# A kernel's index stores: which VectorE operation each waits for, and how far apart they are planned

## The chip, the core and the metric

The kernel runs on one core of one Trainium2 chip. The metric is the device time of one execution in microseconds; the number that stands for a kernel is the median of several executions.

## What is computed

The kernel does two things in a row: a DeltaNet attention block, and a router with two of eight experts for every token.

```python
# attention: B, H, S, D = 4, 8, 768, 48
k_n = k / (norm(k) + 1e-06)
for t in range(S):
    y[:, :, t] = einsum('bhd,bhde->bhe', q[:, :, t], state)
    v_old = einsum('bhde,bhd->bhe', state, kt)
    state = state + bt * einsum('bhd,bhe->bhde', kt, vt - v_old)
# router and experts: x is y as 3072 tokens x 384; E = 8 experts, F = 1024
noisy_logits = x @ w_gate + log1p(exp(x @ w_noise)) * noise
top2 = argpartition(-noisy_logits, 2, axis=1)[:, :2]
top2_w = softmax over the two
for e in range(E):
    out[mask_e] += top2_w[mask_e] * (maximum(x[mask_e] @ w1[e], 0) @ w2[e])
```

The recurrence over tokens is done in chunks of 64 tokens, so that it becomes small matmuls and the inversion of small triangular matrices. Which tokens an expert gets depends on the data, so the tokens' rows are sorted by expert in DRAM: a list `tokens_x` says, for every place of every expert, the token's number, its weight and where its row of `x` lies.

## The kernel before

**Attention.** There are 24 units: 6 steps of 4 units, a unit being one chunk of 64 tokens of two batch entries with all 8 heads. For a unit, TensorE turns k and q (L614), multiplies k by k, q by k and the state by k (`by_token`, L630), reads the state with q (L903), solves for the new values (L948), adds up the state (L970), finishes the answer (L1007), turns it (L1017) and multiplies it by the router's weights (L1022). GpSimd scales v by the norms of k (L912). VectorE masks the product of q and k (`within`, L882), subtracts what the state already gives from v (`recur`, L932), adds the new state (`add_state`, L982), and inverts the triangular matrices of a step: a column at a time, a product (L761) and an addition (L765). ScalarE copies most results out of PSUM. The rows of the answer are stored to `rows_y` by SP (`store`, L399).

**Routing.** When all steps of a group are through (3, 2 and 1 steps: `ROUTES`), `route` works out for its tokens both experts, both weights and both places in `tokens_x` (the last of it is the cast to integers at L1153). Then the lists are stored: for each unit and each of the two experts one indirect DMA by GpSimd writes 128 entries of 12 bytes to their places in `tokens_x` (`spread`, L441). These are the *index stores*: 24 for the first group, 16 for the second, 8 for the last, 48 in all.

**Early experts.** Expert 0's weights fit beside the attention. After steps 2 and 4, SP loads the first entries of expert 0's list (`early_rows`, `early_meta`, L1278), which waits for the stores of these steps; GpSimd gathers those tokens' rows (`take_rows`, L405); and TensorE computes expert 0 for them (`early`, L1322, L1343, L1367), two tiles of 128 tokens as batch 1, then three as batch 2.

**Experts.** After the attention, `rest` does what is left of expert 0 (L1731 to L1757), and experts 1 to 7 follow (L1591 and L1702). For each, GpSimd gathers rows, adds up weights (L1557) and adds the results to the output in DRAM (L460).

**What sets the order.** The attention, the routing and the early experts aren't emitted in the order of the code. Every operation is a job with an engine, an estimated cost, the things it reads and writes, and perhaps a due time. `Jobs.order` plans all of them on a model of the five engines and returns them by planned start; then they are emitted in this order, and each engine's queue runs them in it, GpSimd's and SP's too. Before the plan, due times are handed back from a job to what it needs. Jobs with `apart` may not be planned to start closer together than that: `spaced` holds the earliest start of the next such job. Index stores of the first two groups have `apart=jobs.APART` (L1231), the last group's have none (`paced` is false for the last step).

**What a store waits for.** `spread` gets a list `behind` and makes the store wait for each instruction in it ("not all of them at once", L452). The list is `columns`, which `column` (L765) replaces with the addition of the inversion's column that was emitted last. So a store waits until VectorE has done the last column operation planned ahead of it. Once the last inversion has been emitted, the list no longer changes.

Of the kernel before, what the change touches and what calls it, by code (L numbers as in the profile page):

```python
# [100 lines left out]
class Jobs:  # L101
# [122 lines left out]
        return sorted(done, key=lambda job: job.start)  # L224

    AFTER = -20
    APART = 1.6
    PATIENCE = 0.112
    SOON = 44.8

# [7 lines left out]
def kernel(  # L238
# [39 lines left out]
    nc = tc.nc  # L278
# [191 lines left out]
    def deltanet(ictx):  # L470
# [6 lines left out]
            [psum.tile([128, 2, 512], FP32, name=f"pair{i}") for i in range(3)],  # L477
        )
        PE, ACT, DVE, POOL, SP = Jobs.ENGINES

        def bank(size, ahead=False):

            if size == 2:
                return Bank(2, (0, 1) if ahead else (0, 1, 2))
            return Bank(1, (0,) if ahead else (0, 1))
# [55 lines left out]
        def t_invs(g):  # L541
            return t_two[g % 2]
# [82 lines left out]
        def by_token(out, to, kT, rhs):  # L625

            for j in range(NP):
                for b in range(2):
                    for z in range(2):
                        nc.tensor.matmul(  # L630
                            out[to(z, b), z, j], kT[rows_of[z], j, crossed(z, b)],
                            rhs(z, j, b), start=(j == 0), stop=(j == NP - 1),
                            skip_group_check=True,
                        )
# [52 lines left out]
        def invert(g):  # L687

            first_s, steps = INVERSIONS[g]
            t, v_ = t_invs(g)[:, 0:steps], nc.vector  # L690
            t_key, d_key, n_key, ss_key, root_key = (
                (x, g % 2) for x in ("t", "d", "norm", "ss", "root")
            )
            diagonal = t.rearrange("p s i j -> p s (i j)")[:, :, 0 : Q * Q : Q + 1]
            ss, root, norm, d, minus_d = (x(g)[:, 0:steps] for x in small.values())
            shape = [128, steps, Q, Q]
            soon = FIRST + first_s * PACE + 2 * steps + 1.0
            per = 1.06 * steps

            def squares():  # L700
                v_.tensor_copy(ss, diagonal)
                v_.tensor_scalar_max(root, ss, 1e-30)

            def by_log():
                nc.scalar.activation(root, root, ACTF.Ln)
                nc.scalar.activation(root, root, ACTF.Exp, scale=0.5)

            def lengths():


                v_.reciprocal(norm, root)
                v_.tensor_tensor(out=norm, in0=norm, in1=ss, op=ALU.mult)
                v_.tensor_tensor(out=norm, in0=norm, in1=root, op=ALU.add)
                v_.tensor_scalar(
                    out=norm, in0=norm, scalar1=0.5, scalar2=1e-6, op0=ALU.mult, op1=ALU.add
                )
                v_.tensor_tensor(out=d, in0=norm, in1=norm, op=ALU.mult)
                v_.reciprocal(d, d)
                v_.tensor_tensor(
                    out=d, in0=d, in1=beta_b[:, first_s : first_s + steps], op=ALU.mult  # L720
                )
                v_.tensor_scalar_mul(minus_d, d, -1.0)

            jobs.add(DVE, 0.4, squares, reads=[t_key], writes=[ss_key, root_key], due=soon)
            jobs.add(ACT, 0.5, by_log, writes=[root_key], due=soon + 1)

            for x in range(steps):
                jobs.add(
                    POOL, 1.5,
                    lambda x=x: [nc.gpsimd.affine_select(  # L730
                        out=t[:, x], in_=t[:, x], pattern=[[1, Q], [-1, Q]], base=0,
                        channel_multiplier=0, compare_op=ALU.is_gt, fill=0.0,
                    )],
                    reads=[ss_key], writes=[t_key], due=soon + 3,
                )
            every_beta = [("beta", i) for i in range(128 // H)]
            jobs.add(
                DVE, 2.0, lengths, reads=[root_key, ss_key, *every_beta], writes=[n_key, d_key],
                due=soon + 3,
            )  # L740
            for x in range(steps):
                jobs.add(
                    DVE, 0.2,
                    lambda x=x: v_.transpose(out=norms(first_s + x), in_=norm[:, x]),  # L744
                    reads=[n_key], writes=[("norms", first_s + x)],
                )
            jobs.add(
                DVE, 0.15 + per,
                lambda: v_.tensor_tensor(
                    out=t, in0=t, in1=minus_d[:, :, None, :].to_broadcast(shape), op=ALU.mult  # L750
                ),
                reads=[d_key], writes=[t_key],
            )


            def column(j):
                shape = [128, steps, Q - 1 - j, j]
                part = parts[:, 0 : steps * shape[2] * j].rearrange(
                    "p (s i j) -> p s i j", s=steps, j=j
                )  # L760
                v_.tensor_tensor(  # L761
                    out=part, in0=t[:, :, j + 1 :, j, None].to_broadcast(shape),
                    in1=t[:, :, None, j, 0:j].to_broadcast(shape), op=ALU.mult,
                )
                columns[:] = [v_.tensor_tensor(  # L765
                    out=t[:, :, j + 1 :, 0:j], in0=t[:, :, j + 1 :, 0:j], in1=part, op=ALU.add
                ).ins]

            for j in range(1, Q - 1):
                jobs.add(  # L770
                    DVE, 0.36 + 0.0019 * steps * j * (Q - 1 - j), lambda j=j: column(j),
                    writes=[t_key, *(("column", first_s + x, j) for x in range(steps))],
                )
            jobs.add(DVE, 0.2, lambda: v_.memset(diagonal, 1.0), writes=[t_key])
            jobs.add(
                DVE, 0.15 + per,
                lambda: v_.tensor_tensor(
                    out=t, in0=t, in1=d[:, :, :, None].to_broadcast(shape), op=ALU.mult
                ),
                reads=[d_key], writes=[t_key],  # L780
            )
# [86 lines left out]
        def within(n):  # L868

            turned(n, "q", qps, NQ, qTs, NQ)  # L870
            p = bank(2, True)
            jobs.add(
                PE, 0.6,
                lambda: by_token(
                    two_banks(p, C), crossed, kTs(n),
                    lambda z, j, b: qTs(n)[rows_of[z], j, rows_of[b]],
                ),
                reads=[("kT", n % NT_), ("qT", n % NQ)], opens=p, lands=2.0,
            )
            jobs.add(  # L880
                DVE, 0.7,
                lambda: nc.vector.tensor_tensor(  # L882
                    out=qks(n), in0=two_banks(p, C),
                    in1=mask[:, None, None, :].to_broadcast([128, 2, NP, C]), op=ALU.mult,
                ),
                writes=[("qk", n % NQ)], closes=p,
            )

        def recur(n):
# [29 lines left out]
            if c:  # L919
                p_b = bank(2)  # L920
                jobs.add(
                    PE, 0.5,
                    lambda: by_token(
                        two_banks(p_b, D), straight, kTs(n),
                        lambda z, j, b: old[rows_of[z], b, j],
                    ),
                    reads=[("kT", n % NT_), ("st", z, c % N_ST)], opens=p_b,
                )
                r = by_parity(v_n)
                jobs.add(  # L930
                    DVE, 0.58,
                    lambda: nc.vector.tensor_tensor(  # L932
                        out=r, in0=r, in1=two_banks(p_b, D), op=ALU.subtract
                    ),
                    writes=v_key, closes=p_b,
                )
                jobs.add(
                    PE, 0.55, of_state,
                    reads=[("qT", n % NQ), ("qk", n % NQ), ("st", z, c % N_ST)],
                    writes=[("of_state", z)], opens=p_y,  # L940
                )
# [37 lines left out]

            def add_state():  # L980
                if c:
                    nc.vector.tensor_tensor(  # L982
                        out=new, in0=two_banks(p_s, D), in1=old, op=ALU.add
                    )
                else:
                    nc.vector.tensor_copy(new, two_banks(p_s, D))

# [71 lines left out]
                writes=[("logits", turn_r % 2, at + i)], closes=p_xt,  # L1059
            )  # L1060

        columns = []
        small = {
            x: ring([128, most_steps, Q], x, 2) for x in ("ss", "root", "norm", "d", "minus_d")
        }
# [12 lines left out]
        def route(g):  # L1078
# [141 lines left out]
            for x in range(units):  # L1220
                of, i = first_s + x // US, x % US
                for y, to in enumerate(slot):
# [7 lines left out]
                        due=FIRST + (s + paced) * PACE + BEHIND + jobs.AFTER,  # L1230
                        apart=jobs.APART * paced,  # L1231
                    )
# [693 lines left out]
```

## Time and profile before

| | |
|---|---|
| median of 3 runs | 830.22 us (827.91, 830.22, 830.33) |
| profiled execution: its own time | 829.14 us |
| profiled execution: span from the first to the last instruction | 827.3 us |
| TensorE busy | 732.1 us, 88% of the span |
| VectorE, ScalarE, GpSimd busy | 541.8, 308.6 and 418.5 us |
| mean granted TensorE clock | 0.877 of full |
| index stores (L441): issue time on GpSimd | 48, 48.5 us, 1010 ns each |
| gathers of rows for experts (L405, `xr`) | 49, 55.7 us, 1138 ns each |
| stretch of the first group's stores | 216 to 279 us |
| second and last group's stores | 299 to 320 us, 347 to 357 us |
| batch 1 and batch 2 of the early experts on TensorE | 331 to 353 us, 353 to 386 us |

How to read it: times on a page are microseconds of one profiled execution from the start of its span. An engine's name stands for its queue; "L1591" is the line of the kernel. PE is TensorE, PEld its weight loads, DVE is VectorE, ACT is ScalarE, POOL is GpSimd and SP issues DMAs. In the slices of the span each digit is the busy share of one fortieth, 20.7 us, in tenths, and the row PEclk is the clock that TensorE was granted, in tenths of full speed. In a timeline a row ends with how long the engine was idle before it and what ended that. "issue" means that the engine waited for nothing that the profile shows. "remote" is a semaphore event whose sender the profile doesn't name. One matmul of the program shows as two in the trace.

### The profile page before, as it was taken

Reading aid. Unit: us, or ns where it says so; the run is one execution under the profiler, and the core shown is the slowest. Engines: PE = TensorE matmul, PEld = TensorE weight load, DVE = VectorE, ACT = ScalarE, POOL = GpSimd, SP = SyncE. Lnnn points to the kernel's source line nnn. Section 1 sums busy time; section 2 is a strip of 40 time slices with the busy share of each in tenths; the row PEclk is TensorE's granted clock in tenths of the full one; section 3 lists DMA queues with packets and bytes.
Section 4 is the critical chain, followed back from the end, with each engine's and each line's share of the span. In section 5 each row is a group of like instructions: output and inputs, shape, how many; then the busy total and the mean of one; then the engine's idle time right before and its main releaser. Section 6 shows DMA issues by size and latency. Waiting matters only on the chain.

```text
span 827.3 us, 22382 instructions
## 1 busy us (share of the span) xinstructions
PE 732.1 (88%) x9319; PEld 572.1 (69%) x9319; DVE 541.8 (65%) x1100; ACT 308.6 (37%) x728; POOL 418.5 (51%) x408
## 2 busy tenths in 40 slices
PE   5656879898887875999999999999999999999993
PEld 3445768687776765777659668678588587596593
DVE  7999968998762240302588488487586686785831
ACT  3758485856442621222250250430520521501500
POOL 5030031021245343359678777786886886787032
PEclk8556886987575775999999999999999999999997
DMA  4456544322433100525834545444544446333031
GB/s 70 89 99 179 137 130 97 85 61 61 128 70 89 51 23 12 191 60 90 199 103 118 119 113 122 127 111 100 148 148 75 120 139 128 88 61 42 2 39 24
DMA packets 142719, 79.60 MB, mean 96 GB/s; under 512 B 118352, under 2 KB 139024, under 8 KB 141584
## 3 DMA queue, kind: packets, MB, share of 16 engines
q1 hardware_dynamic: 125840, 57.25, 26.6%
q0 software_dynamic: 12800, 19.80, 13.4%
q8 instruction: 75, 1.23, 0.6%
q10 hardware_dynamic: 3968, 1.03, 0.6%
q14 instruction: 36, 0.29, 0.1%
HBM read 49.85 MB, written 20.03 MB: 84 GB/s over the span
## 4 chain that ended last, share of the span: by engine, by line
PE 65%; DVE 15%; issue 11%; POOL 3%; ACT 2%; SPq 2%; DMA 1%; another core or an unknown queue 0%; POOLq 0%; DVEq 0%; ACTq 0%
PE inner L1591 25%; PE outer L1591 14%; DVE w2e L761 5%; PE pair L1343 3%; PE pair L1367 3%; PE pair L630 3%; DVE w1e L765 3%; POOL out_dram L460 2%; DVE w2e L765 2%; PE pair L903 2%; PE inner L1702 2%; PE single L1022 2%; PE pair L948 2%; PE pair L1007 2%; PE pair L970 1%
## 5 line engine op out<-in xcount | busy, mean ns | idle before, releaser
L1658 ACT ACTIVATE hT<-inner 128x416 f32<-128x416 f32 x112 | 57.8, 517 | 260.9 <-PE inner L1591 258.1
L1652 DVE TENSOR_TENSOR hT<-hT,inner 128x416 f32<-128x416 f32 x182 | 105.5, 586 | 63.5 <-PE inner L1591 55.4
L460 POOL DMA_INDIRECT out_dram<-sums,metas_x x51 | 83.4, 1635 | 93.0 <-DVE sums L1491 67.3
L441 POOL DMA_INDIRECT tokens_x<-meta,slot x48 | 48.5, 1010 | 63.4 <-DVE w2e L765 25.9
L1591 PE MATMUL inner<-s_x,w1e 128*128 128x416 f32 x196 | 78.7, 512 | 0.0
L912 POOL TENSOR_TENSOR v<-v,norms 128x384 f32<-128x384 f32 x24 | 23.4, 988 | 104.8 <-DVE norms L744 49.9
L405 POOL DMA_INDIRECT xr<-rows_y,metas_x x49 | 55.7, 1138 | 19.1 <-issue 12.8
L1647 ACT ACTIVATE hT<-hT 128x416 f32<-128x416 f32 x112 | 59.9, 547 | 12.1 <-DVE hT L1652 7.0
L1591 PEld LDWEIGHTS inner<-s_x,w1e 128*128 128x128 f32 x196 | 37.2, 190 | 31.2 <-issue 28.8
L1591 PE MATMUL inner<-xe,w1e 128*128 128x416 f32 x140 | 58.1, 513 | 0.0
L1591 PE MATMUL outer<-t_w,hT 128*128 128x192 f32 x336 | 58.0, 326 | 0.0
L1591 PE MATMUL inner<-s_x,s_w 128*128 128x416 f32 x140 | 56.9, 512 | 0.0
L1591 PEld LDWEIGHTS outer<-t_w,hT 128*128 128x128 f32 x336 | 55.2, 190 | 0.0
L1557 POOL TENSOR_TENSOR w1e<-w1e 128x256 f32<-128x256 f32 x63 | 52.7, 846 | 2.4
L1591 PE MATMUL outer<-w2e,hT 128*128 128x192 f32 x280 | 50.7, 328 | 0.3
L1591 PEld LDWEIGHTS outer<-w2e,hT 128*128 128x128 f32 x280 | 46.1, 190 | 4.3 <-issue 2.1
L1591 PEld LDWEIGHTS inner<-s_x,s_w 128*128 128x128 f32 x140 | 26.6, 190 | 22.3 <-issue 22.3
L819 ACT COPY w<-tt_tb 32x256 f32<-32x256 f32 x96 | 38.6, 402 | 7.1 <-DVE tt_tb L796 3.9
L1591 PEld LDWEIGHTS inner<-xe,w1e 128*128 128x128 f32 x140 | 26.4, 190 | 20.7 <-issue 17.0
L1591 PE MATMUL outer<-t_w,s_h 128*128 128x192 f32 x224 | 40.6, 329 | 0.0
L1487 DVE TENSOR_SCALAR sums<-outer,metas_x 128x192 f32<-128x192 f32 x70 | 27.8, 410 | 18.4 <-PE outer L1591 17.8
L1591 PEld LDWEIGHTS outer<-t_w,s_h 128*128 128x128 f32 x224 | 36.6, 190 | 4.2 <-issue 4.2
(202 smaller groups left out, 1611.3 us busy)
## 6 DMA issues: line engine op xcount, KB each, us to landing
w1e<-in_moe_w_dram SPq DMA_DIRECT2D x8, 1536.0 KB
w2e<-in_moe_w_dram SPq DMA_DIRECT2D x8, 1536.0 KB
v<-in_v_dram SPq DMA_DIRECT2D x48, 96.0 KB
qp<-in_q_dram SPq DMA_DIRECT2D x48, 96.0 KB
out_dram<-empty SPq DMA_DIRECT2D x4, 1152.0 KB
rows_y<-y SPq DMA_DIRECT2D x24, 192.0 KB
xq<-xr SPq DMA_DIRECT2D x52, 84.0 KB
kp<-in_k_dram SPq DMA_DIRECT2D x88, 48.0 KB
```

The source lines that it names most:

```text
L405: d = nc.gpsimd.indirect_dma_start(out=got, out_offset=None, in_=rows_y[0 : units * 128], in_offset=bass.IndirectOffsetOnAxis(ap=index, ax ...
L441: d = nc.gpsimd.indirect_dma_start(out=tokens_x, out_offset=bass.IndirectOffsetOnAxis(ap=slot, axis=0), in_=meta, in_offset=None, bounds_c ...
L460: d = nc.gpsimd.indirect_dma_start(out=out, out_offset=bass.IndirectOffsetOnAxis(ap=index, axis=0), in_=got, in_offset=None, bounds_check= ...
L761: v_.tensor_tensor(out=part, in0=t[:, :, j + 1 :, j, None].to_broadcast(shape), in1=t[:, :, None, j, 0:j].to_broadcast(shape), op=ALU.mult,)
L765: columns[:] = [v_.tensor_tensor(out=t[:, :, j + 1 :, 0:j], in0=t[:, :, j + 1 :, 0:j], in1=part, op=ALU.add).ins]
L819: lambda rows=rows, cols=cols, w64=w64, tt=tt: nc.scalar.copy(w64[rows, :, cols], tt[rows]),
L1487: nc.vector.tensor_scalar_mul(got, p, gate)
L1557: engine.tensor_tensor(out=block(to), in0=block(x), in1=block(y), op=ALU.add if sign == "+" else ALU.subtract,)
L1591: nc.tensor.matmul(p, lhsT, rhs, start=opens and i == 0, stop=i == len(products) - 1, skip_group_check=True,)
L1647: nc.scalar.activation(h, h, ACTF.Relu)
L1652: nc.vector.tensor_tensor(out=h, in0=h, in1=p, op=ALU.add if sign > 0 else ALU.subtract)
L1658: nc.scalar.mul(h, p, float(sign))
```

## The change

The list that stores wait behind is no longer fed by the inversion's columns alone. A helper `passed` puts a finished instruction into it, and four kinds of VectorE operation call it, each replacing what was there before: the column's addition, the masking of q times k, the subtraction from v, and the addition of the state (but for the first chunk, where the state is only copied). A store thus waits for the last operation of these four kinds that was planned ahead of it. VectorE's other operations (routing, transposes, the early experts' scaling) don't call it. The second edit sets the planned distance of two stores of the first two groups from 1.6 to 2.4.

```diff
     AFTER = -20
-    APART = 1.6
+    APART = 2.4
...
         PE, ACT, DVE, POOL, SP = Jobs.ENGINES
+
+        columns = []
+
+        def passed(done):
+            columns[:] = [done.ins]
...
-                columns[:] = [v_.tensor_tensor(
+                passed(v_.tensor_tensor(
                     out=t[:, :, j + 1 :, 0:j], in0=t[:, :, j + 1 :, 0:j], in1=part, op=ALU.add
-                ).ins]
+                ))
...
-                lambda: nc.vector.tensor_tensor(
+                lambda: passed(nc.vector.tensor_tensor(
                     out=qks(n), in0=two_banks(p, C),
                     in1=mask[:, None, None, :].to_broadcast([128, 2, NP, C]), op=ALU.mult,
-                ),
+                )),
...
-                    lambda: nc.vector.tensor_tensor(
+                    lambda: passed(nc.vector.tensor_tensor(
                         out=r, in0=r, in1=two_banks(p_b, D), op=ALU.subtract
-                    ),
+                    )),
...
-                    nc.vector.tensor_tensor(
+                    passed(nc.vector.tensor_tensor(
                         out=new, in0=two_banks(p_s, D), in1=old, op=ALU.add
-                    )
+                    ))
...
-        columns = []
         small = {
```

In the built program VectorE's instructions stand in the same order as before up to the early experts. On GpSimd's queue, the scaling of v stands further ahead among the first group's 24 stores: units 18 and 19 after stores 3 and 4 (before: 4 and 5), units 20 to 23 after stores 12, 12, 15 and 15 (before: 16, 17, 21 and 22); on SP's queue the first load of `early_meta` stands behind two more stores of answer rows; and on TensorE's queue the first early-expert operations stand some matmuls later, with other PSUM banks.

## Prediction

> **What bounds the kernel now.** I read the page first, then the chain that ended last in order of time, then the timelines of GpSimd, TensorE and VectorE around the index stores (L441), and last a table of TensorE by stages.
>
> ```profile
> span 827.3 us, 22382 instructions
> ...
> PE   5656879898887875999999999999999999999993
> ...
> PEclk8556886987575775999999999999999999999997
> ```
>
> From slice 17 on (331 us) TensorE is full at full clock, and the chain names little but its matmuls as far as 738 us: the early experts from 331, expert 0 from 388.6, experts 1 to 7 from 404.5. What starts earlier there ends earlier. The change acts before 357 us, where TensorE has holes. These are the chain's pieces around the largest one (start, us, what):
>
> ```profile
> 300.00 0.91 PE pair L630 x39
> 300.91 0.81 PE single L1017 x6
> ...
> 303.97 1.11 issue
> 305.07 0.33 PE pair L630 x4
> 305.40 1.09 issue
> ...
> 320.26 1.86 issue
> 322.12 1.68 PE pair L903 x52
> ```
>
> TensorE waits for nothing that the profile shows, yet starts 4 matmuls and stands still for 1.1 us. GpSimd meanwhile issues 16 stores without a pause (first and last shown):
>
> ```profile
> 299.38 1.02 POOL L441 DMA_INDIRECT tokens_x<-meta,slot  x1 [12.28 <-DVE r_d L1095]
> ...
> 318.76 0.98 POOL L441 DMA_INDIRECT tokens_x<-meta,slot  x1 [0.30 <-issue]
> ```
>
> VectorE's last subtraction of the recurrence comes after both:
>
> ```profile
> 322.29 0.55 DVE L932 TENSOR_TENSOR v<-v,pair 128x384 f32<-128x384 f32 x1 [15.06 <-remote]
> ```
>
> TensorE by stages (stage, length, busy us (starts), clock, DMA share, GB/s):
>
> ```profile
> 248.70:255.20 6.50, 3.88 (x45) 0.50 0.02 1
> ...
> 301.70:322.10 20.40, 7.28 (x53) 0.60 0.02 1
> 322.10:331.10 9.00, 8.91 (x205) 0.58 0.08 26
> 345.20:357.20 12.00, 11.97 (x46) 1.00 0.02 1
> ```
>
> In 20.4 us 53 matmuls start, against 205 in the 9 us after. 248.7 to 255.2, under six stores 1.3 us apart, looks the same. DMA engines are 2% busy, so no bandwidth is short. The last row has eight stores too, yet TensorE stays full: those are the early experts' matmuls, 0.22 to 0.33 us each. So back-to-back index stores starve TensorE of *small* matmuls. The cause I can't see; I count it as observed.
>
> [...] a store occupies GpSimd 0.98 us, while the load of `early_meta`, which waits for the stores, starts 2.9 us after the last one (279.10 to 281.98). [...] after both stalls the clock reads 0.50 (322.1 to 326).
>
> **The change, part by part.** VectorE's and ScalarE's work keeps its order up to the early experts. I therefore take the new waits from the built program and the times from the old trace.
>
> *What a store costs.* From the gaps between TensorE's starts: a store over 1.6 us after the previous one leaves one gap of 0.35 to 0.45 us (237.93 and 239.61); one right behind another costs about 1.2 more. Stores 11 to 16 (245.7 to 254.0) left gaps of 5.6 us, 17 to 21 3.5, 22 0.6, the pair at 276.8 1.2, the two row gathers at 284.7 2.1; stores 1 to 10 (216 to 240.6) 7.4. Sum up to 300 us: 20.4 us.
>
> *First group with the change.* Old: store 11 waited for the last column operation, stores 12 to 24 for no VectorE work at all. New: store 4 waits for the subtraction ending 230.87, 8 and 9 for 245.11 and 245.43, 10 to 12 for 255.97, 258.35, 259.96, 15 for 276.67, 16 for 280.93, 19 and 20 for 284.90 and 288.76, 23 for 298.16, 24 for 301.08 (old times). Still back to back: 8-9, 13-14, 16-17-18, 20-21-22. Of stores 1 to 23, 17 stand alone or head a run (0.4 each, 6.8) and six follow (1.2 each, 7.2); store 12, only 1.6 behind store 11, gets 0.4 more: 14.4. Store 24 and the gathers fall into the next part. Gain 20.4 - 14.4 = 6.0 us if all of it is on the path. It is not: behind store 4 stands unit 19's multiplication of v (229.77), now 1 to 2 us later, and VectorE's next subtraction and columns behind it. I take 4.5; bounds 1 and 8 (all on the path, and a higher clock after shorter stalls).
>
> *What else queues behind the waits.* v of units 20, 21 stands behind store 12, but needs the very next VectorE operation (260.08): nothing. v of units 22, 23 stands behind store 15, up to 10 us later than 268.18, needed at 300.5: hidden by 20 us. On SP the first `early_meta` load moves behind two y stores (done by 298): nothing. It waits for store 24, so the gathers of early rows move from 284.7 to T+6.9, T being the subtraction at 301.08: 1.3 for the store, 2.9 to the load, 2.7 to the gather (281.98 to 284.70). They were needed at 327.9.
>
> *Second group.* All 16 stores wait for the last subtraction (old 322.29), planned spacing or not: no marked VectorE operation follows it. They stand behind the gathers, so they run from T+9.6 to T+30 (20.4 us, as before), instead of T-1.7 to T+18.7. It is still one run, but no longer in front of the last subtraction. TensorE now has T to T+7.5 undisturbed. Old: small work ends T+30.2 (331.26). At the clock of 1.00 shown at 300.2 to 301.7 a group of 32 takes 0.68 us; counting L630, L1022, L903, L948, L1007, L948 and their ScalarE copies, some 65 matmuls are left at T+7.5. Under the run they start at 8 per us beside the gathers (16 in 2.0 us), 5 per us in the first 6 us of stores (20 in 3.9, 30 in 6.2), then about 2 (20 in 12.7): small work ends near T+24, 6 us earlier. Then come early-expert matmuls, which eight stores did not slow; sixteen may: I take off 2.5. Tail gain 3.5; bounds -4.3 and 8.
>
> *What is late next.* Rows of tiles 2 to 4: `early_meta` T+33, gathers T+36, landed about T+44; batch 1 takes 21.8 us (331.26 to 353.07), so batch 2 would start about T+48.5, not held. The last eight stores follow the same logits; expert 0's rows were gathered by 373.8 and used at 387: about 10 us of slack. *The spacing of 2.4 itself* is a number of the planner and no wait: it moves stores behind v's multiplications on GpSimd's queue, which is busy 40.6 of the 105 us from 215 to 320, and the first `early_meta` load on SP. I cost it at nothing beyond what stands above; were the 20 us of cover before 300.5 gone, each store ahead of a v would cost its 1.3 us.
>
> **Sum.** 829.14 (profiled execution, 1.1 below the median 830.22 and inside 827.91 to 830.33) - 4.5 - 3.5 = 821.1; on the median 822.2. I say 822.
>
> **Rivals.**
> *Whole tail gained:* small work is done before the run bites, and the rows' landing at T+44 sets batch 2, 8 us before 353.07. With 5 from the first group: 830.2 - 13 = 817. For it: only some 65 small matmuls are left. Against: the gathers disturb TensorE at once, as at 284.9.
> *Slower:* the run of 2 + 16 meets too much small work. Its place is T+7.5 to T+32.4 (TensorE resumed 2.4 us after the last store, at 322.12), 2.2 us later than small work ends now; it carries about 19 + 30 + 34 = 83 matmuls. With more than 83 left (132 if TensorE is at half clock, 1.04 us per 32), the rest follows at T+34.5, 4.3 us later than now. If followers and the later v let the first group gain only 1, the end is 830.2 + 3.3 = 833.5. For it: sixteen stores remain unspaced. Against: the clock before T.
> *The stores only change places:* the 1.2 us per follower is paid anyway (14.4 against 20.4 is within my counting), or stalls have another cause: 829 to 831.
>
> **Chances.** Likeliest 0.50, whole tail 0.15, slower 0.22, only moved 0.13. About 0.3% (2.5 us) is what a measurement of this kernel can tell from no change. Faster: 0.50 and 0.15 nearly whole, 0.66; same 0.12; slower 0.22. The likeliest alone spans 819 to 826 (first group 1 to 8, tail at its value); with the rivals, leaving out a tenth on each side, 813 to 832.
>
> **What would show it.** Right: the 249-255 and 265-269 trickle of L630 and L839 shrinks; the last subtraction follows the one before it by some 2 us, not 21; the 16 stores begin after it; L1343 starts near 320, batch 2 near 345; nothing in experts 1 to 7 changes length. Wrong: L1343 starts at 331 or later with TensorE in pieces beside the 16 stores (slower rival); batch 2 waits for rows (whole tail); TensorE trickles with no store near (other cause).

## The result, and the profile after

| | before | after |
|---|---|---|
| median, of 4 runs each | 830.28 us (827.91 to 839.67) | 822.24 us (817.59 to 825.89) |
| profiled execution: own time, span | 829.14, 827.3 us | 825.89, 824.1 us |
| early experts' first product on TensorE | 331.10 us | 327.20 us |
| batch 2's first product | 354.35 us | 351.30 us |
| first product of expert 1 | 404.46 us | 400.95 us |

The ratio is 0.988, with a 95% interval from 0.984 to 0.993. Ratios leave out executions more than 1.5% longer than the fastest of the same kernel. So the change made the kernel faster here, by about 8 us in the median. The four times after lie in two pairs, 817.6 and 818.6, 825.9 and 825.9, and the profiled execution belongs to the higher pair. The page of after answers to the first lines shown of before:

```profile
span 824.1 us, 22389 instructions
...
PE   5656888887788862999999999999999999999993
...
PEclk8556788888677685999999999999999999999997
```

TensorE is still full from slice 17 on. The hole ahead of it hasn't gone: slice 16 (309 to 330 us) now has a 2. The chain of after, in order of time, says what the hole is made of:

```profile
303.70 1.11 PE pair L1012 x32
...
306.75 0.19 PE single L1027
306.93 16.02 issue
322.96 0.90 PE single L1022 x3
```

TensorE stands for 16 us in one piece, where it stood for 1.1 us at a time before. GpSimd's timeline has the second group's 16 stores in just that stretch (first and last), again 1.3 us apart:

```profile
302.21 1.02 POOL L441 DMA_INDIRECT tokens_x<-meta,slot  x1 [0.30 <-issue]
...
321.58 0.98 POOL L441 DMA_INDIRECT tokens_x<-meta,slot  x1 [0.31 <-issue]
```

VectorE's timeline has the last two subtractions of the recurrence. They are 2.4 us apart instead of 21.8, and both lie ahead of the run, as the change asks:

```profile
293.08 0.56 DVE L937 TENSOR_TENSOR v<-v,pair 128x384 f32<-128x384 f32 x1 [0.75 <-PE pair L635]
...
295.48 0.56 DVE L937 TENSOR_TENSOR v<-v,pair 128x384 f32<-128x384 f32 x1 [0.65 <-POOL meta L1179]
```

Why TensorE stands still is seen on ScalarE (its timeline from 303 to 323):

```profile
303.95 0.48 ACT L1050 COPY xT<-single 128x384 f32<-128x384 f32 x1 [0.31 <-remote]
322.43 0.48 ACT L1038 COPY y<-pair 128x384 f32<-128x384 f32 x1 [18.00 <-remote]
```

The copy at 322.43 takes the result of the 32 matmuls of L1012, which had started at 303.70. TensorE's next work (L1022) needs that copy and follows it at once, at 322.96. Of the semaphores that this copy waits for, only TensorE's own changes in these 18 us, at 322.40; so what is late comes from TensorE and is neither a buffer nor a store. There was almost no small work left to hold up: one hand-over from TensorE to ScalarE took 18 us.

The kernel before has such a hand-over too. Its last subtraction (L932) starts at 322.29 after 15.06 us of waiting. The 32 matmuls that it needs had all been started 12.9 us earlier; this is the last of them:

```profile
309.39 0.31 PE L630 MATMUL pair<-st,kT 64*64 64x48 f32 x1 [0.50 <-issue]
```

There, too, TensorE's semaphore moves only at 322.2 to 322.3. What differs is who waits: before, TensorE had other matmuls to start in the meantime; after, it had none. The table by stages (stage, length, busy us and starts, clock, DMA share, GB/s) shows both halves of the result:

```profile
248.70:255.20 6.50, 5.44 (x198) 1.00 0.57 140
302.20:322.60 20.40, 2.46 (x38) 0.52 0.07 17
322.60:331.60 9.00, 7.88 (x29) 0.58 0.59 213
```

The first stretch had 45 starts before and has 198 now. The run of 16 stores had 53 starts in 20.4 us and has 38.

### The profile page after: what moved, and what is told of

The parts are those of the page before. It is cut to its first block, busy times and chain, and to the rows that moved or that the text cites. A ratio compares the mean times of both kernels' runs of the same rounds, so it can differ in the third digit from the quotient of the medians.

```text
span 824.1 us, 22389 instructions
## 1 busy us (share of the span) xinstructions
PE 718.1 (87%) x9319; PEld 561.7 (68%) x9319; DVE 541.7 (66%) x1100; ACT 307.8 (37%) x728; POOL 417.7 (51%) x408
## 3 DMA queue, kind: packets, MB, share of 16 engines
q0 software_dynamic: 12800, 19.80, 13.3%
q8 instruction: 75, 1.23, 0.7%
## 4 chain that ended last, share of the span: by engine, by line
PE 62%; DVE 14%; issue 12%; POOL 4%; ACT 2%; SPq 2%; DMA 1%; another core or an unknown queue 0%; DVEq 0%; POOLq 0%
PE inner L1595 24%; PE outer L1595 12%; DVE w2e L766 4%; PE pair L1347 3%; PE pair L635 3%; PE pair L1371 3%; DVE w1e L770 2%; POOL out_dram L460 2%; PE single L1027 2%; PE pair L1012 2%; PE inner L1706 2%; PE pair L975 2%; PE single L619 2%; DVE w2e L770 1%; PE pair L953 1%
## 5 line engine op out<-in xcount | busy, mean ns | idle before, releaser
L917 POOL TENSOR_TENSOR v<-v,norms 128x384 f32<-128x384 f32 x24 | 23.7, 1008 | 91.1 <-DMA rows_y<-y 44.6
L405 POOL DMA_INDIRECT xr<-rows_y,metas_x x49 | 55.8, 1138 | 19.6 <-issue 12.8
L1595 PEld LDWEIGHTS inner<-s_x,s_w 128*128 128x128 f32 x140 | 26.6, 190 | 22.3 <-issue 22.3
L1595 PE MATMUL outer<-t_w,s_h 128*128 128x192 f32 x224 | 40.6, 329 | 0.0
```

What stands on the lines that cost most here:

```text
L405: d = nc.gpsimd.indirect_dma_start(out=got, out_offset=None, in_=rows_y[0 : units * 128], in_offset=bass.IndirectOffsetOnAxis(ap=index, ax ...
L1595: nc.tensor.matmul(p, lhsT, rhs, start=opens and i == 0, stop=i == len(products) - 1, skip_group_check=True,)
```

## Experiments

Each ratio is to the kernel before, timed beside it on the same chip. The fourth column is the median of the kernel before there.

| run | us, median (range) | ratio, 95% interval | before | first product of the early experts |
|---|---|---|---|---|
| `wait_only` | 823.5 (820.1 to 828.7) | 0.989 (0.985 to 0.993) | 831.2 | 322.85 |
| `apart_only` | 835.8 (829.1 to 844.5) | 1.004 (1.002 to 1.006) | 831.2 | 338.09 |
| `after_again` | 821.1 (814.9 to 826.5) | 0.984 (0.979 to 0.989) | 831.2 | 326.18 |
| `hold` | 816.0 (813.4 to 818.5) | 0.980 (0.976 to 0.983) | 831.2 | 302.17 |
| `double` | 844.8 (840.7 to 855.9) | 1.015 (1.006 to 1.024) | 829.8 | 337.90 |
| `double_oob` | 856.4 (842.1 to 858.3) | none | 829.8 | 361.60 |
| `pool_busy` | 821.3 (814.2 to 832.3) | 0.986 (0.983 to 0.989) | 829.8 | 324.60 |
| `no_second` | 802.4 (801.4 to 804.5) | 0.966 (0.960 to 0.972) | 829.8 | 304.57 |
| `act_marks` | 808.7 (805.9 to 813.4) | 1.016 (1.013 to 1.019) | 796.8 | 297.81 |
| `marks_w` | 807.5 (804.4 to 811.6) | 1.014 (1.010 to 1.017) | 796.8 | 299.70 |
| `no_first` | 791.8 (788.4 to 796.9) | 0.994 (0.992 to 0.996) | 796.8 | not compared |
| `after_third` | 810.7 (805.8 to 813.4) | 1.009 (1.007 to 1.012) | 803.7 | 299.58 |

The runs fell on four chips: the first four in the table on one, the next four on another, three on a third and the last on a fourth. On the first two of them the kernel before takes 830 us, as it did where the result was measured; call these chips A. On the two others it takes 797 and 804 us; call these chips B. Nothing was done to bring that about, and in these runs the sign of the change goes with it. Each chip was also used at another time, and why the chips differ isn't shown.

**Which of the two edits does it.**

```diff
 # wait_only: the changed kernel
...
-    APART = 2.4
+    APART = 1.6
 # apart_only: the kernel before
...
-    APART = 1.6
+    APART = 2.4
```

> The waits of the change alone, with the planned distance of 1.6 as before. My theory (the waits separate the stores, the planned distance costs and brings nothing itself): nearly the whole gain, 819 to 824 us, and the last subtraction of the recurrence (L937) ends by 303 instead of 322. Rival (the distance of 2.4 does it): 828 to 831 us, stores of the first group still in runs of five or more 1.3 us apart.

> The planned distance of 2.4 alone, waiting for the inversion's columns as before. My theory: no gain, 828 to 831 us, because after the last column nothing holds a store and GpSimd issues them as fast as it can, 1.3 us apart; the sixteen stores of the second group still run in front of the last subtraction, which ends near 322. Rival (the distance does it): 819 to 824 us.

> The changed kernel once more, for the spread of its times: its four runs lay at 825.9, 825.9, 818.6 and 817.6 us. I expect both groups of times again. If the difference lies in the stall in front of the 16 stores of the second group, a profile near 818 us has the early experts' first product (L1347) starting near 320 instead of 327, and one near 826 us has it near 327.

The waits alone bring 1.1%, the distance alone costs 0.4%. With the waits there, the distance can't be told from none: 0.984 and 0.989 have intervals that overlap. So the waits carry the gain. That the distance alone makes the kernel slower was missed. In its profile the first group's stores end only 4 us later (283 instead of 279), but the gathers start at 302.3 instead of 284.7. What they wait for is the first load of `early_meta`, which the planned distance has moved behind two more stores of answer rows on SP's queue, as in the changed kernel. Those two stores start at 296.69 and 298.99, when their rows have been computed, and the load only at 299.64 (281.98 before). Behind the gathers the 16 stores run later as well (305.0 to 325.4), with 52 matmuls started in their 20.4 us, as 53 were before, and the early experts start 7 us later. In the changed kernel this place on the queue costs nothing, since there the last store of the group is itself late (293.91, load at 296.96). The changed kernel came out in the same spread of times again; its profile (825.32 us) has the standstill too, with L1347 at 326.18. I have no profile of an execution at 815 to 819 us, so what those escape isn't shown.

**Hold the 16 stores until the small work is over.** Every engine's order stays; only the second group's stores get a wait for ScalarE's last copy of logits.

```diff
-                lambda: nc.scalar.copy(
+                lambda: (passed if s + 1 == NS else id)(nc.scalar.copy(
                     logits(turn_r)[:, at + i],
...
+            if s + 1 == NS:
+                last_copies.append(len(jobs.jobs) - 1)
...
+                    if g == 1:
+                        held_stores.append(len(jobs.jobs) - 1)
...
+            for i in held_stores:
+                jobs.jobs[i].after.update(last_copies)
             jobs.run()
```

> The changed kernel, but the second group's 16 stores also wait for ScalarE's last copy of logits, so that they start only when TensorE has nothing but the early experts' large products left. Every engine's order is unchanged. My theory (back-to-back stores hold up small matmuls and not large ones): no standstill of 16 us after 306.8, L1347 starts near 311 instead of 327, its products keep their length beside the stores, and batch 2 then waits for its rows until about 346 instead of starting at 351.4: 818 to 822 us, and one group of times instead of two. Rival (large matmuls are held up as well by 16 stores): L1347 starts near 311 but in pieces until 332, and the time is 826 us or more. Rival (the standstill has another cause): TensorE still stands still from 307 to 323.

The standstill among the small work is gone, and L1351 (L1347 there) starts 24 us earlier than in `after_again`. The median is 5 us lower, 816.0, below the 818 to 822 that were expected. By the medians a fifth of the 24 us arrives, by the two profiled executions half (825.32 and 813.61), and the timeline of TensorE shows where the rest goes:

```profile
302.17 12.21 PE L1351 MATMUL pair<-early_xe,w1e 128*128 128x256 f32 x42
...
317.56 4.14 PE L1375 MATMUL pair<-w2e,tt_tb 128*128 128x384 f32 x12 [0.94 <-issue]
326.05 9.62 PE L1375 MATMUL pair<-w2e,tt_tb 128*128 128x384 f32 x20 [4.35 <-ACT tt_tb L1362]
335.51 1.04 PE L1330 MATMUL pair<-ident,early_x 128*128 128x128 f32 x6
337.53 0.59 PE L1330 MATMUL pair<-ident,early_x 128*128 128x128 f32 x3 [0.98 <-DMA early_x<-rows_y,early_meta]
```

The first 42 large matmuls run without a gap beside ten stores (0.29 us each). But at 321.7 TensorE runs out of inputs, and ScalarE's timeline has the same kind of late hand-over as above:

```profile
317.13 0.38 ACT L1362 ACTIVATE tt_tb<-pair 128x256 f32<-128x256 f32 x1 [2.48 <-issue]
...
325.62 0.66 ACT L1362 ACTIVATE tt_tb<-pair 128x256 f32<-128x256 f32 x2 [8.01 <-remote]
```

The products it copies at 325.62 had been started by 316. For 6 us after the hole a matmul starts every 0.64 us, half as often as later; the granted clock is 0.50 there. Batch 1 takes 33.0 us from its first start to its last (302.17 to 335.19) where `no_second`, without these stores, needs 23.7 (304.57 to 328.30). So my sentence that large matmuls aren't held up needs a limit: here they ran on for 19.5 us (302.17 to 321.7, with gaps of 0.32 and 0.94 us), until a result was handed over late.

**What in a store holds TensorE up.** Three kernels put something behind each of the first group's 24 stores: a second store into an unused tensor, a second store whose places are all out of range, or 0.93 us of arithmetic on GpSimd.

```diff
 # double: again() is a store like spread()'s, into another tensor, without waits
...
+                            *([again(metas(g)[:, x, y], to[:, x : x + 1])] if g == 0 else []),
 # double_oob: nowhere holds E * N, a place out of range
...
-                            spread(metas(g)[:, x, y], to[:, x : x + 1], of, columns)
+                            spread(metas(g)[:, x, y], slots_x[:, x : x + 1], of, columns)
+                            for slots_x in ((to, nowhere) if g == 0 else (to,))
 # pool_busy
...
+                            *([nc.gpsimd.tensor_tensor(
+                                out=scratch, in0=scratch, in1=scratch, op=ALU.mult
+                            )] if g == 0 else []),
```

> The changed kernel, but each of the first group's 24 stores is followed at once by a second one of the same entries into another DRAM tensor that nothing reads. Every engine's order is otherwise the same. My price: a store right behind another leaves 1.2 us of gaps between TensorE's small matmuls, so 24 x 1.2 = 29 us more of gaps up to the first group's end; most of it on the path: 838 to 850 us, and the last store of the group near 315 to 320 instead of 294. Rival (the gaps are not the stores'): under 826 us.

> As with doubled stores, but the second one's places all lie outside the list, so that GpSimd issues it and none of its entries is written. If TensorE is held up by GpSimd's issuing, the time is that of the doubled stores (838 to 850 us by my price); if by the writes to DRAM, it is that of the changed kernel, 818 to 826 us. I expect the first.

> The changed kernel, but each of the first group's 24 stores is followed by a multiplication of about 1 us on GpSimd over a tile that nothing else uses, in place of a second store. My theory (it is the DMA that holds TensorE up, not a busy GpSimd): 819 to 826 us, with v's multiplications up to 1 us later. Rival (a busy GpSimd as such): 838 us or more, as with doubled stores.

Arithmetic costs nothing: 0.986 against 0.984 for `after_again`. By the ratios a second store costs 1.015 - 0.986, about 24 us, over `pool_busy`, 1.0 us for each of 24. The last store of the group starts at 319.66 instead of 292.40, 27.3 us later with 23 second stores ahead of it, 1.2 us each: the price of the prediction. Out of range there is no sign that it costs less, with executions from 842 to 858 us; they lie too far apart for an interval, and the profile is of the one at 858, so its 361.60 isn't compared. Those entries still moved packets: GpSimd's queue has 13,568 in both kernels, 768 more than in the changed kernel; half of the 768 are of 32 bytes where `double` has 96. So the bytes written are unlikely to matter; whether issuing or the number of packets does was not separated.

**Leave stores out.** Without the second group's:

```diff
                             spread(metas(g)[:, x, y], to[:, x : x + 1], of, columns)
-                        ],
+                        ] if g != 1 else None,
```

> The changed kernel with the second group's 16 stores left out (the tokens of steps 3 and 4 are in no expert's list, so their places stay blank and fewer rows are moved later). My theory: the standstill from 307 to 323 is gone, the early experts' first product starts near 311 instead of 327, and batch 2 near 333 instead of 351: 803 to 810 us. Rival (the standstill has another cause): it stays, and the time is 815 us or more.

The time, 802.4 us, is just below the 803 to 810 that were expected. L1347 starts at 304.57, 13.3 us after the first group's last store. In the changed kernel the same work takes 33.3 us (293.91 to 327.20), so the run of 16 still costs 20 us on chips A.

**Spread three stores among the small work, load weights later, leave the first group out.** `act_marks` lets ScalarE's copies of the last step call `passed`; `marks_w` adds a wait to the load of expert 1's weights; `no_first` leaves out the first group.

```diff
 # act_marks, for the copies of y_n, xT and logits
...
+            last = passed if s + 1 == NS else id
...
-                lambda: nc.scalar.copy(
+                lambda: last(nc.scalar.copy(
 # marks_w: act_marks, and in load_weights
...
+        for i in gathers if e == 1 else ():
+            tc.add_manual_dep(d, i.name, SYNC, reason="early rows first")
 # no_first
...
-                        ],
+                        ] if g else None,
```

> The changed kernel, but in the last step three of ScalarE's copies (the answer, its turned form, the logits) enter the list that stores wait behind, as VectorE's operations do. So the second group's first three stores wait for copies inside the remaining small work and only the fourth for the last copy; every engine's order is unchanged. My theory: against the held stores (ratio 0.980) the run begins about 4 us earlier, the rows of batch 2 land about 4 us earlier, and three stores among the small work cost it 1 to 3 us: 812 to 817 us. Rival (these three hold the small work up as the run did): 818 us or more.

> As the run before it, but the load of expert 1's weights (two loads of 1.5 MB, begun just before the gathers of batch 2's rows) waits until these rows have landed. With the held stores the gathers were issued by 331.7 and the last rows were there only at 337.5, beside 260 GB/s of weights. My theory: rows 2 to 3 us earlier, and 0 to 3 us less in all (810 to 816 us), if TensorE waits for rows; nothing later is late, since the weights are needed from 380 on. Rival (the later weights make GpSimd's sums of weights late): slower by 2 us or more.

> The changed kernel with the first group's 24 stores left out (the tokens of steps 0 to 2 are in no expert's list, fewer rows are moved later, so the total says little). What counts is the time of the last subtraction of the recurrence (L937), 293 to 295 us in the changed kernel. By my prices 14.4 us of gaps are left in the changed kernel up to there: with all of them on the path it ends at 279 to 281; I expect 281 to 286. Rival (spaced stores cost next to nothing): 291 or later.

These fell on a chip B, where the kernel before takes 796.8 us, so my numbers in us don't apply. Two versions of the change are *slower* there than the kernel before, by 1.4 to 1.6%. `marks_w` and `act_marks` can't be told apart. In `no_first` the last subtraction starts at 278.69. On the same chip it starts at 285.88 in `act_marks` and at 288.46 in `marks_w`, whose first groups are those of the changed kernel: 7.2 to 9.8 us for 24 stores, 0.3 to 0.4 each.

**The changed kernel on a chip B.**

> The changed kernel once more, on whichever chip it falls. Chips have differed: the kernel before took 830 to 831 us on two of them and 796.8 us on a third, where TensorE's gaps beside the stores came once in 127 or 128 matmuls instead of in pieces of four. My theory (the gain is the gaps that the waits avoid, the price is rows that land later): on a chip at 830, a ratio of 0.980 to 0.990; on a chip at 797, no gain, since there are few gaps to avoid and batch 2 waits for its rows: 803 to 810 us, ratio 1.008 to 1.016. Rival (the gain does not depend on the gaps): 0.98 to 0.99 on either.

The last run fell on another chip B, and the change made the kernel slower by 0.95%, as expected for such a chip. Its page:

```profile
span 805.2 us, 22389 instructions
...
PE   4656888897786889699999999999999999999993
...
PEclk9556787788888789899999999999999999999997
...
q8 instruction: 75, 1.23, 0.7%
```

The hole of slice 16 is gone (9), though the 16 stores run here too (295.31 to 315.68). The 6 of slice 17 (322 to 342 us) is what is late now: the rows of batch 2. TensorE's timeline:

```profile
299.58 12.31 PE L1347 MATMUL pair<-early_xe,w1e 128*128 128x256 f32 x48
...
312.09 10.57 PE L1371 MATMUL pair<-w2e,tt_tb 128*128 128x384 f32 x32
327.70 0.91 PE L1326 MATMUL pair<-ident,early_x 128*128 128x128 f32 x3 [5.04 <-DMA early_x<-rows_y,early_meta]
```

Batch 1 takes 23 us beside the stores and isn't held up. Then TensorE waits from 322.7 to 331.4, but for nine transposes. The chain shows for what:

```profile
314.70 3.74 DMA tokens_x<-meta,slot
318.51 2.07 DMA early_meta<-tokens_x
...
321.46 0.36 POOL early_x L405
...
324.14 6.46 DMA early_x<-rows_y,early_meta
...
330.74 0.88 PE pair L1326 x3
```

That is the last of the 16 stores, the load of the list, the gathers and their landing. The change put this row of steps behind the first group's last store, which it had moved back (278.12 to 293.91 on chips A). I have no trace of the kernel before on a chip B, so that it doesn't wait there for these rows is concluded from this, not seen.

## Why the prediction was right, and where it wasn't

The time was right (822.2 for 822), for chips A, and in part by luck. In the profiled executions the first group gained more than the sum had and the tail lost where the sum had a gain, so that 3.25 us were gained instead of 8.0. The median is the middle of two pairs, at 818 and 826, and none of the four executions took 822.

*Index stores back to back starve TensorE.* Right on chips A, and now shown by adding stores: 1.0 to 1.2 us for a follower (prediction 1.2). A lone store costs 0.3 to 0.4 us on a chip B; on chips A 0.35 to 0.45 was not tested again. The runs show that such stores hold TensorE up, not by which path.

*First group, 4.5 us, bounds 1 and 8.* Too small: the subtraction that the last store waits for ended at 293.64 instead of 301.07, 7.4 us earlier. My sum priced gaps alone. Gaps over 0.3 us between TensorE's starts went from 26.6 to 22.8 us in all up to that point, 3.8 less. By its records, TensorE's idle time in that stretch stayed as it was (14.1 and 14.5 us); its busy time fell from 71.0 to 63.3 us, with a granted clock of 0.65 and 0.70. The higher clock, an estimate of mine, stood only in the upper bound. Gaps over 0.3 us also have other causes: `no_first` still has some 15 us of them.

*Tail, 3.5 us, small work done at T+24.* This is the step that failed. I let a stock of 65 small matmuls drain at so many per us. In the profiled execution 54 were left at T+7.5, and 38 started under the run, within its first 4.7 us and so faster than I had them; then a single result took 18 us from TensorE to ScalarE. Small work ended at T+33.6, and the tail lost 3.5 us instead of gaining 3.5. So L1347 came 3.9 us earlier and not 11. The median's 8 us includes executions at 818 us that no profile shows. The late hand-over stood in the prediction's own line of the last subtraction (15.06 us of waiting, for matmuls started 12.9 us before): I read it as TensorE starting too few, and so priced starts and no hand-over. The sum was also kind to itself: at its own rates the last 19 of the 65 end at T+25 to T+28, not at T+24.

*2.5 us taken off for large matmuls beside sixteen stores.* Too small on chips A (9.3 us in `hold`), too large on chips B (none). In the profiled execution of the change the term doesn't arise: its large matmuls begin after the last of the stores.

*Rows at T+44, batch 2 not held by them.* On chips A batch 2 followed batch 1 without a wait (349.85). On chips B the small work takes 12.8 us (286.7 to 299.6), and batch 2 waits for its rows, which are there at T+44, T being 286.7: the landing itself was as predicted. The rival "whole tail gained" had this bound but priced it from chips A, where it is still a gain.

*The distance of 2.4 at nothing.* Right beside the waits; alone it costs 0.4%, by the load of `early_meta` that it moves on SP's queue. That move was seen and taken to be free, for a last store that is late. The 40.6 us for GpSimd's queue in that part of the prediction are the index stores alone; with all its work GpSimd is busy 48.0 of those 105 us.

*Experts 1 to 7.* Unchanged: what was gained at L1347 is there at expert 1 (3.5 us) and at the end (3.25).

An assumption behind all this failed as well: that one chip's gaps are the kernel's. The change buys fewer stalls with later rows. Where stalls are dear it is 1.2 to 1.6% faster, where they are cheap 0.95% slower. On chips A `hold` is the best kernel measured with all its work, 5 us below the changed kernel by the median, with intervals that overlap; on chips B, where `hold` and `wait_only` were not run, none that I ran beats the kernel before with all its work done.

## What to carry to other kernels

When an engine stops without a reason that the trace names, don't count only the instructions left in front of the stall: look for the one result that another engine waits for, and compare the time at which it was started with the time at which it was used. One late hand-over cost 16 us here; at the mean rate of the kernel before under its 16 stores (53 in 20.4 us) that is the time of some 40 matmuls. A wait that spaces out transfers also delays what follows them, so name the consumer and its slack, and price both sides. Look at what an edit moves on every queue: alone, the planned distance made the kernel slower through one load on SP's. Time such an edit on more than one chip before keeping it: here the same change made the kernel 1.2% faster on one and 1% slower on another.

## What the runs showed of the hardware

*Two kinds of gaps.* On chips A TensorE beside stores advances in pieces of about four matmuls. `double` at 260 us, on TensorE's timeline:

```profile
260.70 0.33 PE L646 MATMUL pair<-st,kT 64*64 64x48 f32 x4 [0.42 <-issue]
261.44 0.33 PE L646 MATMUL pair<-st,kT 64*64 64x48 f32 x4 [0.41 <-issue]
262.19 0.34 PE L646 MATMUL pair<-st,kT 64*64 64x48 f32 x5 [0.42 <-issue]
262.90 0.47 PE L646 MATMUL pair<-st,kT 64*64 64x48 f32 x4 [0.38 <-issue]
```

In the four traces of chips B it doesn't. There the gaps between TensorE's starts that are over 0.5 us and that no named wait ends lie far apart: counting matmuls from one to the next gives 128, 254, 127, 256, 128, 127, 128, 382 and 127 for `after_third`, all near multiples of 127.5. Eight of these gaps follow the same matmul, counted from the program's start, in `after_third` and `act_marks`, so they go with places in the program. What TensorE waits for there isn't shown: the page above counts 75 packets, 1.23 MB, on a queue named "instruction", but no trace ties a gap to one of them. The ten gaps of `after_third` between 214 and 288 us are 0.8 to 3.5 us long, 18.7 us together. They don't need stores: `no_first` has eight at such places, 0.6 to 2.7 us long, 10.5 us together, and `act_marks`, with the stores and on the same chip, nine, 14.0 us together. That is about half of the 7.2 us that lie between these two at the last subtraction. Nor are they peculiar to chips B: in the changed kernel's profile on a chip A the five longest gaps between 215 and 294 us that no named wait ends stand at such places (128, 127, 254 and 639 matmuls apart), 1.1 to 2.1 us long, 8.3 us together. So chips A have both kinds, and where the pieces of four come from stays open.

*Late hand-overs.* In `after` and `hold`, ScalarE waits 18.00 and 8.01 us for results that TensorE had started at 303.70 and by 316. Its copies, at 322.43 and 325.62, come at about the end of a run of stores (the last one's issue ends at 322.56 and 323.17). In each of the ten traces of chips A, that of the kernel before among them, ScalarE or VectorE waits at least once between 210 and 345 us for more than 1.5 us until TensorE's semaphore moves, with no TensorE work that ended just then (15.06 us in the kernel before, 18.00 in `after`, 8.01 in `hold`); in the four traces of chips B they never do. Whether the products or their signals were late stays open.

*Weights beside rows.* The last gathered rows took 6.8 us from the gather to their use while 3 MB of weights came in (`act_marks`, 322.89 to 329.66), and 3.5 us when the weights waited for them (`marks_w` on the same chip, 324.67 to 328.14).
